# First slot's weights sent a step ahead of their split, routing reads ordered ahead, and the plan of the rest drawn up in the second slot

## The chip, the core and the metric

The kernel runs on one core of a Trainium2 chip. The metric is device time in microseconds (us) of one execution. Engines are named as the profile names them: PE (matmuls), PEld (its weight loads), DVE (vector), ACT (scalar), POOL (GpSimd) and SP (which here only issues transfers and reads indices into registers; its queue is SPq in the profile).

## The reference

Three stages in a row, all in float32:

```
# 1. gated linear attention, B=4, H=8, S=768, D=48
f = 1 / (1 + exp(-f_logit))
state = f[t] * state + k[t] (x) v[t];   y[t] = q[t] @ state
# 2. dense layer over 3072 tokens of 384 (d_ff 2048)
x = softplus(y @ w_in) @ w_out
# 3. mixture of 8 experts, one expert for each token (F=1024)
e = argmax(x @ w_gate + modality_bias[modality_id]);  p = softmax(...)[e]
out = p * (relu(x @ w1[e]) @ w2[e])
```

## The kernel before, in words

**Stages one and two.** Attention and the dense layer run in 128 steps, `NG` = 8 groups of 384 tokens by 16 blocks of 128 hidden columns. Each step is an `up` (L573), a softplus on ACT and DVE, and a `down` (L653) into three accumulators `x2ps0` to `x2ps2`. When a group is done, `route1` reads the three accumulators: the gate's logits `lg` on DVE, and the rows of tokens `rows`, of which parts 0 and 2 are read on ACT and part 1 on DVE. `route2` then finds each token's expert and its place, and POOL scatters the rows into a buffer in HBM, `xs`, sorted by expert (L724).

**Stage three** works in slots. A slot is up to 256 tokens of one expert, and `seq` lists them: four "first" slots, whose experts are known from `plan_first` before the last group is done, and then the "rest", which `plan_rest` finds once all tokens are counted. Slots are numbered from 0 here, so slot 3 is the last of the first four and slot 4 the first of the rest. A slot has eight blocks f0 to f7 of `m_up`, nine matmuls each into one of `HBUF` = 4 PSUM buffers `h` (L1115). A block's result is read twice, by ACT (`hh`, L1117) and by DVE (`hl`, L1118), and only then is its buffer free for the block four later. Two `m_down` follow, 24 matmuls each (L1138), and `m_out` scales the accumulator on ACT (`o`, L1147) and scatters it on POOL (L1148).

**Weights.** While a slot runs, the next slot's weights are fetched (`m_weights`): eight loads of 384 KB, turn by turn of w1 and w2, each into one of `RAW` = 6 buffers `raw` (two for slot 0). Each is then split in two: ACT casts it to a high half (`w1h`, `w2h`, L1009), DVE subtracts for a low half (`w1l`, `w2l`, L1010). I call the eight loads of a slot A to H in the order of issue: A, C, E and G are w1, B, D, F and H are w2. Between B and C, SP issues the load of the slot's token rows, `xr` (L984). Before the loads SP reads the expert's number (`woff`, L994), and before `xr` the row's offset (`roff`, L982). Both come out of the plan on DVE. For a slot of the rest, `xr` also waits for every scatter of rows and for all eight "pads" to have landed (`after` in `m_load`); pads are the transfers of 388 KB by which POOL closes each expert's rows (`pad_rows`, L1209).

**Order.** Each engine runs its instructions in the order that a scheduler wrote when the program was built, from the kernel's program order and from its own idea of when data arrive. `follow(a, b)` adds an order without a wait: a stands behind b if both are on one engine. `at(s, f)` runs f at step s of the dense layer. `m_slots` is given calls to place: `(2, 2): then` draws up the plan of the rest in block 2 of slot 2.

Of the kernel before, what the change touches and what calls it, by code (L numbers as in the profile page):

```python
# [7 lines left out]
F32 = mybir.dt.float32  # L8
# [3 lines left out]
AF = mybir.ActivationFunctionType  # L12
ALU = mybir.AluOpType
# [5 lines left out]
NT, DM, DFF = 3072, 384, 2048  # L19
E, FE = 8, 1024  # L20
TG = 384
NG = NT // TG
# [3 lines left out]
SLOT = 256  # L26
# [9 lines left out]
PRE = 4  # L36
# [3 lines left out]
TAIL = "uaduue"  # L40
WPOS = 1
PADROW = E * CAP
PAIR0, PAIR1 = NF, NF * (NG - 1)
RW = 388
BIG = 65536.0
WS = 256.0
# [5 lines left out]
def moe_chain(ctx, tc, qT, kT, fT, vp, w_in, w_out, mod, w_gate, mbias, w1, w2, out):  # L52
    nc = tc.nc
# [23 lines left out]
    x2ps = [ps_x.tile([128, 512], F32, name=f"x2ps{j}") for j in range(3)]  # L77


    def follow(ins, other):  # L80

        tc.add_manual_dep(ins.ins, other.name,
                          mybir.DependencyInfo(mybir.DependencyClass.NoSync, mybir.DependencyReason.DATA),
                          reason="first steps first")

    def behind(ins):
        follow(ins, anchor[0])

    marks = {}
# [315 lines left out]
    biasT = cp.tile([128, 24, 8], F32, name="biasT")  # L405
# [261 lines left out]
    def sm(nm, shape, dt=F32):  # L667
        return gp.tile(shape, dt, tag=nm, name=nm)

    def route1(G, j):  # L670
        if j == 0:
            rt[G] = {"lg": sm("lg", [128, 3, 8]), "rows": gp.tile([128, 3, RW], F32, tag="rows", name="rows", bufs=1)}
        lg, rows = rt[G]["lg"], rt[G]["rows"]
        nc.vector.scalar_tensor_tensor(lg[:, j, :], x2ps[j][:, DM:DM + 8], 1.0 / WS, biasT[:, 3 * G + j, :],
                                       op0=ALU.mult, op1=ALU.add)
        if j == 1:
            nc.vector.tensor_scalar(rows[:, j, 0:DM], x2ps[j][:, 0:DM], 1.0 / WS, None, op0=ALU.mult)
        else:
            nc.scalar.activation(rows[:, j, 0:DM], x2ps[j][:, 0:DM], AF.Copy, scale=1.0 / WS)  # L679

    def route2(G):
        d = rt[G]
# [55 lines left out]
    def pick(nm, num, w, offs):  # L738
# [16 lines left out]
        nc.vector.tensor_reduce(row, tmp, axis=AX.X, op=ALU.add)  # L755
        nc.vector.tensor_scalar(roff, row, float(PADROW), None, op0=ALU.add)
        return woff, roff, beg, end
# [34 lines left out]
    def halves(num, offs):  # L792
# [15 lines left out]
        nc.vector.tensor_copy(pw, ph[:, :, 0])  # L808
        nc.vector.tensor_scalar(pr, ph[:, :, 1], float(PADROW), None, op0=ALU.add)
        return pw, pr  # L810
# [48 lines left out]
    def late_consts():  # L859
# [9 lines left out]
        nc.gpsimd.iota(etab, pattern=[[0, 2], [1, 8]], base=0, **it)  # L869
        nc.gpsimd.iota(rows0, pattern=[[0, 2], [CAP, 8]], base=-PADROW, **it)  # L870
        nc.gpsimd.iota(snum, pattern=[[0, 1]], base=0, channel_multiplier=1, allow_small_or_imprecise_dtypes=True)
# [3 lines left out]
    def pad_out():  # L875
        behind(nc.scalar.dma_start(xs[PADROW:PADROW + SLOT, :].rearrange("(p j) w -> p j w", j=2),
                                   padt.unsqueeze(1).to_broadcast([128, 2, RW])))
# [3 lines left out]
    def at(s, f):  # L881
        extra.setdefault(s, []).append(f)
# [32 lines left out]
    for u in range(4, 33):  # L915
        G, j = divmod(u, 4)
        t = 3 * u - 10 if u < 8 else 4 * u - 19
# [63 lines left out]
    def m_load(s, where, i, n):  # L981
        ro = nc.sync.value_load(plans[where][1][i:i + 1, 0:1], min_val=0, max_val=PADROW)  # L982
        xr = xrp.tile([128, 2, RW], F32, tag="xr", name="xr")[:, 0:n, :]
# [8 lines left out]
    def m_weights(s, woff, i, whole):  # L992

        wo = nc.sync.value_load(woff[i:i + 1, 0:1], min_val=0, max_val=E - 1)  # L994
        pl = m1p[s % 2]
        names = ("w1h", "w1l", "w2h", "w2l")
        w1h, w1l, w2h, w2l = wts[s] = [pl.tile([128, 3 * FE], F32R, tag=n, name=n) for n in names]
        ops = []
        for n in range(4):
            for src, hi, lo in ((w1, w1h, w1l), (w2, w2h, w2l)):  # L1000
                def op(n=n, src=src, hi=hi, lo=lo):
                    c = slice(768 * n, 768 * n + 768)
                    rows = src[bass.ds(wo, 1), :, c].rearrange("o p f -> p (o f)")
                    if whole and src is w1:
                        nc.sync.dma_start(hi[:, c].bitcast(F32), rows)
                        return
                    t = rawp.tile([128, 768], F32, tag="raw", name="raw")
                    nc.sync.dma_start(t, rows)
                    nc.scalar.copy(hi[:, c], t)  # L1009
                    nc.vector.tensor_tensor(lo[:, c], t, hi[:, c].bitcast(F32), op=ALU.subtract)  # L1010
                ops.append(op)
        return ops

    def p_load(s):
        xr = xrp.tile([128, 2, RW], F32, tag="xr", name="xr")[:, 0:1, :]
        for n in range(2):
            ro = nc.sync.value_load(plans["rest"][3][0:1, n:n + 1], min_val=0, max_val=PADROW)
            ins = nc.sync.dma_start(xr[HALF * n:HALF * n + HALF, 0, :], xs[bass.ds(ro, HALF), :]).ins
# [83 lines left out]
    def m_up(s, f):  # L1102
        d = sl[s]
        t = d["t"]
        w1h, w1l = (t.rearrange("p (k f) -> p k f", k=3) for t in wts[s][0:2])
        if f == 0:
            d["hh"] = mp.tile([128, NF2, SLOT], F32R, tag="hh", name="hh")
            d["hl"] = mp.tile([128, NF2, SLOT], F32R, tag="hl", name="hl")
        if d["n"] == 2:
            hp = ps_h.tile([128, TG], F32, tag="h", name="h")  # L1110
            fs = slice(128 * f, 128 * f + 128)
            n = 0
            for kd in range(3):
                for w, x in ((w1h, 0), (w1h, 1), (w1l, 0)):
                    nc.tensor.matmul(hp[:, 0:SLOT], w[:, kd, fs], t[x][:, kd, :], start=(n == 0), stop=(n == 8))  # L1115
                    n += 1
            nc.scalar.activation(d["hh"][:, f, :], hp[:, 0:SLOT], AF.Relu)  # L1117
            nc.vector.scalar_tensor_tensor(d["hl"][:, f, :], hp[:, 0:SLOT], 0.0, d["hh"][:, f, :].bitcast(F32),  # L1118
                                           op0=ALU.max, op1=ALU.subtract)
        elif f % 2 == 0:  # L1120
            w1f = wts[s][0].bitcast(F32).rearrange("p (k f) -> p k f", k=3)
            hp = ps_h.tile([128, 2, 128], F32, tag="h", name="h")
            for i in range(2):
                fs = slice(128 * (f + i), 128 * (f + i) + 128)
                for kd in range(3):
                    nc.tensor.matmul(hp[:, i, :], w1f[:, kd, fs], t[:, kd, :], start=(kd == 0), stop=(kd == 2))
            hh, hl = d["hh"][:, f:f + 2, 0:128], d["hl"][:, f:f + 2, 0:128]
            nc.scalar.activation(hh, hp, AF.Relu)
            nc.vector.scalar_tensor_tensor(hl, hp, 0.0, hh.bitcast(F32), op0=ALU.max, op1=ALU.subtract)
# [26 lines left out]
    seq = [("first", i, 2) for i in range(NPRE)] + [("rest", i, 2 if i < NA else 1) for i in range(NSTAT)]  # L1156
# [4 lines left out]
    def m_slots(items, last):  # L1161

        for x, (s, it) in enumerate(items):
            nxt = items[x + 1] if x + 1 < len(items) else None
            wops = []
            if nxt:
                wops = m_fetch(*nxt)
            for f in range(NF2):
                if it[0] == "pair":
                    if f % 2 == 0:  # L1170
                        p_up(s, f)
                elif f >= ahead or s:
                    m_up(s, f)
                if (s, f) in last:
                    last[s, f]()
                if wops:
                    wops.pop(0)()
                if f == 6 and nxt:
                    m_T(nxt[0], (0,) if it[2] == 2 else (0, 1))
            if x + 2 < len(items) and items[x + 2][1][0] == "pair":  # L1180
                for op in p_weights(items[x + 2][0], w1):
                    op()
            for j in range(it[2]):
                if it[0] == "pair":
                    p_down(s)
                else:
                    m_down(s, j)
                if j == 0 and it[2] == 2 and nxt:
                    m_T(nxt[0], (1,))
            if s == len(seq) - 3:  # L1190
                follow(nc.gpsimd.drain(), gone[-1])
# [14 lines left out]
    def pad_rows(e):  # L1206
# [5 lines left out]
            tc.declare_no_dep(ins, other, reason="rows of different experts")  # L1212
        pads.append(ins)

    def pre():
        plans["first"] = plan_first()
        for i in range(NPRE - 1):
            m_load(i, "first", i, 2)
        for n, op in enumerate(m_fetch(0, seq[0])):
            at(16 * (NG - 1) + PRE + 1 + n, op)  # L1220

    ffn(0, 16 * (NG - 1) + 3)
    for p in (ap1, ap2, ps_r, ps_h):
# [31 lines left out]
    seq = list(enumerate(seq))  # L1255
# [2 lines left out]
        for e in range(E):  # L1258
            pad_rows(e)

    m_slots(seq, {(0, 3): final, (1, 2): lambda: route2(NG - 1), (1, 4): ready, (2, 2): then, (6, 3): limits})
    def slow():
        sp = cp
        ma, mb = m1p[0], m1p[1]
# [182 lines left out]
```

## Time and profile before

| | us |
|---|---|
| three runs | 814.3, 816.16, 819.37 |
| median | 816.16 |
| profiled execution, whole | 814.61 |
| its span, first to last instruction | 812.9 |
| PE busy | 786.5 (97%) |
| DVE busy | 633.5 (78%) |
| ACT busy | 530.4 (65%) |

Times in the text are in us from the start of the span. The profiled execution lies at the lower end of the three runs, 1.55 us under their median. The four first slots lie in 556 to 635 us of the span; the matmuls end at 807.5.

### The profile page before, as it was taken

How to read it: one execution, taken by the hardware profiler on the slowest of the kernel's cores; microseconds unless marked ns; L12 is line 12 of the kernel's file. 1: busy time of each engine (PE TensorE's matmuls, PEld its weight loads, DVE VectorE, ACT ScalarE, POOL GpSimd, SP SyncE). 2: the span in 40 equal slices, each digit the busy share in tenths (PEclk: the TensorE clock that was granted, in tenths of full speed). 3: DMA queues.
4: the chain of work that ended last, by engine and by line, in shares of the span. 5: the costliest groups of instructions: out<-in, count | busy, mean ns of one | idle time of the engine just before them, and what ended most of it. 6: DMA issues, size and time to landing. Idle time of an engine off the chain costs nothing.

```text
span 812.9 us, 16010 instructions
## 1 busy us (share of the span) xinstructions
PE 786.5 (97%) x5878; PEld 730.8 (90%) x5878; DVE 633.5 (78%) x1265; ACT 530.4 (65%) x1057; POOL 64.9 (8%) x86
## 2 busy tenths in 40 slices
PE   4899999999999999999999999999999999999997
PEld 4656568999999999999999999989999999999987
DVE  6899999998888888888888866888886766666131
ACT  5787797767766676777676665566775656655242
POOL 2000000200010010010010010100042111000010
PEclk9999999999999999999999999999999999999999
DMA  8794221321132132122221010055598976673980
GB/s 292 255 328 140 59 67 44 91 73 54 45 95 58 45 98 58 51 85 61 62 75 38 23 38 8 30 161 171 200 352 298 309 226 216 213 225 119 366 311 16
DMA packets 53976, 110.84 MB, mean 136 GB/s; under 512 B 7655, under 2 KB 27930, under 8 KB 53888
## 3 DMA queue, kind: packets, MB, share of 16 engines
q1 hardware_dynamic: 48768, 96.61, 37.2%
q0 software_dynamic: 4160, 12.67, 4.2%
q8 instruction: 48, 0.79, 0.4%
q10 hardware_dynamic: 960, 0.44, 0.2%
q14 instruction: 40, 0.33, 0.1%
HBM read 91.92 MB, written 13.65 MB: 130 GB/s over the span
## 4 chain that ended last, share of the span: by engine, by line
PE 49%; DVE 23%; ACT 10%; issue 10%; DMA 7%; SPq 1%; POOL 1%; POOLq 0%; DVEq 0%; ACTq 0%
PE x2ps L653 11%; PE h L573 11%; PE x2ps L1138 10%; PE h L1115 10%; DVE l L637 3%; DVE w L636 2%; DMA raw<-in_w_dram 2%; ACT e L633 1%; DVE f L110 1%; PE r L206 1%; ACT e L622 1%; DVE lo L640 1%; DVE am L214 1%; DVE l L639 1%; ACT r L623 1%
## 5 line engine op out<-in xcount | busy, mean ns | idle before, releaser
L573 PE MATMUL h<-xh,wih 128*128 128x384 f32 x336 | 118.4, 352 | 1.2 <-DVE e L587 1.2
L653 PE MATMUL x2ps<-woh,hi 128*128 128x392 f32 x336 | 115.3, 343 | 1.8 <-ACT hi L612 1.5
L653 PE MATMUL x2ps<-wol,hi 128*128 128x392 f32 x336 | 114.5, 341 | 0.0
L573 PE MATMUL h<-xh,wil 128*128 128x384 f32 x336 | 113.5, 338 | 0.0
L653 PE MATMUL x2ps<-woh,lo 128*128 128x392 f32 x336 | 113.4, 341 | 0.0
L573 PE MATMUL h<-xl,wih 128*128 128x384 f32 x336 | 113.3, 337 | 0.0
L1115 PE MATMUL h<-thl,w1h 128*128 128x256 f32 x528 | 96.5, 284 | 0.0
L1010 DVE TENSOR_TENSOR w2l<-raw,w2h 128x768 fp32r<-128x768 f32 x56 | 53.2, 951 | 38.8 <-ACT w2h L1009 18.0
L1115 PEld LDWEIGHTS h<-thl,w1h 128*128 128x128 f32 x528 | 82.0, 190 | 0.0
L638 ACT CAST hi<-l 128x768 fp32r<-128x768 f32 x48 | 40.0, 834 | 54.1 <-DVE l L637 42.5
L1115 PE MATMUL h<-thl,w1l 128*128 128x256 f32 x264 | 74.3, 282 | 0.0
L1138 PE MATMUL x2ps<-w2h,hh 128*128 128x384 f32 x208 | 71.0, 341 | 0.2 <-ACT rows L679 0.2
L1138 PE MATMUL x2ps<-w2h,hl 128*128 128x384 f32 x208 | 70.1, 337 | 0.8 <-DVE hl L1118 0.8
L1138 PE MATMUL x2ps<-w2l,hh 128*128 128x384 f32 x208 | 69.9, 336 | 0.0
L573 PEld LDWEIGHTS h<-xh,wih 128*128 128x128 f32 x336 | 63.0, 188 | 4.9 <-DVE e L587 2.0
L724 POOL DMA_INDIRECT xs<-rows,pos x24 | 27.1, 1129 | 504.4 <-DVE w L635 166.3
L653 PEld LDWEIGHTS x2ps<-woh,hi 128*128 128x128 f32 x336 | 63.0, 188 | 3.2 <-ACT hi L612 2.6
L653 PEld LDWEIGHTS x2ps<-woh,lo 128*128 128x128 f32 x336 | 63.0, 188 | 0.5
L573 PEld LDWEIGHTS h<-xl,wih 128*128 128x128 f32 x336 | 63.3, 188 | 0.0
L653 PEld LDWEIGHTS x2ps<-wol,hi 128*128 128x128 f32 x336 | 63.1, 188 | 0.0
L573 PEld LDWEIGHTS h<-xh,wil 128*128 128x128 f32 x336 | 63.0, 188 | 0.0
L1010 DVE TENSOR_TENSOR w1l<-raw,w1h 128x768 fp32r<-128x768 f32 x48 | 45.8, 954 | 21.9 <-ACT w1h L1009 21.3
(275 smaller groups left out, 1826.7 us busy)
## 6 DMA issues: line engine op xcount, KB each, us to landing
raw<-in_w_dram SPq DMA_DIRECT2D x104, 384.0 KB
f<-in_f_dram SPq DMA_DIRECT2D x28, 192.0 KB
k<-in_k_dram SPq DMA_DIRECT2D x28, 192.0 KB
q<-in_q_dram SPq DMA_DIRECT2D x28, 192.0 KB
xr<-xs SPq DMA_DIRECT2D x12, 388.0 KB
v<-in_v_dram SPq DMA_DIRECT2D x32, 144.0 KB
w1h<-in_w_dram SPq DMA_DIRECT2D x12, 384.0 KB
xf<-y SPq DMA_DIRECT2D x48, 72.0 KB
```

The lines of the kernel that those rows point to most:

```text
L110: nc.vector.tensor_tensor_scan(d["f"], d["f"], clampt.to_broadcast([128, TG]), 1.0 if first else fl[:, n:n + 1], op0=ALU.mult, op1=ALU.min)
L206: nc.tensor.matmul(pa[h][:, cs], d["k"][64 * h:64 * h + 64, cs], d["q"][64 * h:64 * h + 64, cs], start=(c == 0), stop=True, skip_group_che ...
L214: marks["mask"] = nc.vector.tensor_tensor(am, pa[h][:, 0:TG].rearrange("p (c t) -> p c t", c=3), mask.unsqueeze(1).to_broadcast([128, 3, 1 ...
L573: nc.tensor.matmul(hp, w, x, start=(n == 0), stop=(n == len(terms) - 1))
L636: nc.vector.tensor_tensor(w, w, e, op=ALU.subtract)
L637: nc.vector.tensor_tensor(g, r, g, op=ALU.add)
L638: nc.scalar.copy(hi, g)
L653: nc.tensor.matmul(x2ps[j][:, 0:DM + 8], g[:, ts], w, start=(i == 0 and n == 0), stop=(i == NF - 1 and n == len(terms) - 1))
L724: ins = nc.gpsimd.indirect_dma_start(out=xs, out_offset=bass.IndirectOffsetOnAxis(ap=pos[:, j:j + 1], axis=0), in_=rows[:, j, :], in_offse ...
L1010: nc.vector.tensor_tensor(lo[:, c], t, hi[:, c].bitcast(F32), op=ALU.subtract)
L1115: nc.tensor.matmul(hp[:, 0:SLOT], w[:, kd, fs], t[x][:, kd, :], start=(n == 0), stop=(n == 8))
L1138: nc.tensor.matmul(acc[:, 0:DM], g[:, f, ts], w[:, f, :], start=(f == 0 and n == 0), stop=(f == NF2 - 1 and n == 2))
```

## The change

It has three parts. (1) In slot 0's fetch, a load and its split are two calls, and the split is placed one step behind the load (`m_weights` returns `parts`, `pre` places both). (2) `route1` keeps its reads in `marks`, and in slot 0 blocks f4 to f6 of `m_up` are ordered behind them: `hh` and `hl` of f4 behind the reads of part 0, `hl` of f5 behind those of part 1, `hh` and `hl` of f6 behind those of part 2. (3) `plan_rest` is called in block 6 of slot 1, not in block 2 of slot 2.

```diff
--- before.py
+++ after.py
@@ -40,6 +40,7 @@
 TAIL = "uaduue"
 WPOS = 1
 PADROW = E * CAP
+LATE = 4
 PAIR0, PAIR1 = NF, NF * (NG - 1)
 RW = 388
 BIG = 65536.0
@@ -667,16 +668,21 @@
     def sm(nm, shape, dt=F32):
         return gp.tile(shape, dt, tag=nm, name=nm)
 
+    marks["route"] = []
+
     def route1(G, j):
         if j == 0:
             rt[G] = {"lg": sm("lg", [128, 3, 8]), "rows": gp.tile([128, 3, RW], F32, tag="rows", name="rows", bufs=1)}
         lg, rows = rt[G]["lg"], rt[G]["rows"]
-        nc.vector.scalar_tensor_tensor(lg[:, j, :], x2ps[j][:, DM:DM + 8], 1.0 / WS, biasT[:, 3 * G + j, :],
-                                       op0=ALU.mult, op1=ALU.add)
+        ins = [nc.vector.scalar_tensor_tensor(lg[:, j, :], x2ps[j][:, DM:DM + 8], 1.0 / WS, biasT[:, 3 * G + j, :],
+                                              op0=ALU.mult, op1=ALU.add)]
         if j == 1:
-            nc.vector.tensor_scalar(rows[:, j, 0:DM], x2ps[j][:, 0:DM], 1.0 / WS, None, op0=ALU.mult)
+            ins.append(nc.vector.tensor_scalar(rows[:, j, 0:DM], x2ps[j][:, 0:DM], 1.0 / WS, None, op0=ALU.mult))
+            eng = (0, 0)
         else:
-            nc.scalar.activation(rows[:, j, 0:DM], x2ps[j][:, 0:DM], AF.Copy, scale=1.0 / WS)
+            ins.append(nc.scalar.activation(rows[:, j, 0:DM], x2ps[j][:, 0:DM], AF.Copy, scale=1.0 / WS))
+            eng = (0, 1)
+        marks["route"] = [(j, e, x) for e, x in zip(eng, ins)] + [y for y in marks["route"] if y[0] != j]
 
     def route2(G):
         d = rt[G]
@@ -1006,8 +1012,15 @@
                         return
                     t = rawp.tile([128, 768], F32, tag="raw", name="raw")
                     nc.sync.dma_start(t, rows)
-                    nc.scalar.copy(hi[:, c], t)
-                    nc.vector.tensor_tensor(lo[:, c], t, hi[:, c].bitcast(F32), op=ALU.subtract)
+
+                    def parts():
+                        nc.scalar.copy(hi[:, c], t)
+                        nc.vector.tensor_tensor(lo[:, c], t, hi[:, c].bitcast(F32), op=ALU.subtract)
+
+                    if s:
+                        parts()
+                    else:
+                        return parts
                 ops.append(op)
         return ops
 
@@ -1114,9 +1127,13 @@
                 for w, x in ((w1h, 0), (w1h, 1), (w1l, 0)):
                     nc.tensor.matmul(hp[:, 0:SLOT], w[:, kd, fs], t[x][:, kd, :], start=(n == 0), stop=(n == 8))
                     n += 1
-            nc.scalar.activation(d["hh"][:, f, :], hp[:, 0:SLOT], AF.Relu)
-            nc.vector.scalar_tensor_tensor(d["hl"][:, f, :], hp[:, 0:SLOT], 0.0, d["hh"][:, f, :].bitcast(F32),
-                                           op0=ALU.max, op1=ALU.subtract)
+            two = [None, nc.scalar.activation(d["hh"][:, f, :], hp[:, 0:SLOT], AF.Relu)]
+            two[0] = nc.vector.scalar_tensor_tensor(d["hl"][:, f, :], hp[:, 0:SLOT], 0.0, d["hh"][:, f, :].bitcast(F32),
+                                                    op0=ALU.max, op1=ALU.subtract)
+            if s == 0 and f >= LATE and f < LATE + 3:
+                for j, e, x in marks["route"]:
+                    if j == f - LATE:
+                        follow(two[e], x.ins)
         elif f % 2 == 0:
             w1f = wts[s][0].bitcast(F32).rearrange("p (k f) -> p k f", k=3)
             hp = ps_h.tile([128, 2, 128], F32, tag="h", name="h")
@@ -1212,12 +1229,15 @@
             tc.declare_no_dep(ins, other, reason="rows of different experts")
         pads.append(ins)
 
+    turn = []
+
     def pre():
         plans["first"] = plan_first()
         for i in range(NPRE - 1):
             m_load(i, "first", i, 2)
         for n, op in enumerate(m_fetch(0, seq[0])):
-            at(16 * (NG - 1) + PRE + 1 + n, op)
+            at(16 * (NG - 1) + PRE + 1 + n, lambda op=op: turn.append(op()))
+            at(16 * (NG - 1) + PRE + 2 + n, lambda: turn.pop(0)())
 
     ffn(0, 16 * (NG - 1) + 3)
     for p in (ap1, ap2, ps_r, ps_h):
@@ -1258,7 +1278,7 @@
         for e in range(E):
             pad_rows(e)
 
-    m_slots(seq, {(0, 3): final, (1, 2): lambda: route2(NG - 1), (1, 4): ready, (2, 2): then, (6, 3): limits})
+    m_slots(seq, {(0, 3): final, (1, 2): lambda: route2(NG - 1), (1, 4): ready, (1, 6): then, (6, 3): limits})
     def slow():
         sp = cp
         ma, mb = m1p[0], m1p[1]
```

The scheduler makes of it the following. On PE, DVE, ACT and SP nothing stands in another place before slot 0's blocks.

ACT in slot 0. `hh_6544<-h_...` are the blocks f0 to f7, `thl` is slot 1's transposed tokens, `rows` are route1's reads. Before, from f3 on:

```order
L1117 ACTIVATE hh_6544<-h_6640 128x256
L1117 ACTIVATE hh_6544<-h_6664 128x256
L1117 ACTIVATE hh_6544<-h_6680 128x256
L1117 ACTIVATE hh_6544<-h_6696 128x256
L1099 CAST thl_6712<-r_6713 128x512
L1117 ACTIVATE hh_6544<-h_6720 128x256
L679 ACTIVATE rows_6653<-x2ps0_89 128x384
L1099 CAST thl_6712<-r_6765 128x256
L679 ACTIVATE rows_6653<-x2ps2_91 128x384
```

and in the change:

```order
L1130 ACTIVATE hh_6544<-h_6640 128x256
L1130 ACTIVATE hh_6544<-h_6680 128x256
L1112 CAST thl_6712<-r_6713 128x512
L1130 ACTIVATE hh_6544<-h_6720 128x256
L683 ACTIVATE rows_6653<-x2ps0_89 128x384
L1130 ACTIVATE hh_6544<-h_6664 128x256
L1112 CAST thl_6712<-r_6765 128x256
L683 ACTIVATE rows_6653<-x2ps2_91 128x384
L1130 ACTIVATE hh_6544<-h_6696 128x256
```

f4 (`h_6664`) and f6 (`h_6696`) moved behind the reads of x2ps0 and x2ps2; f5 and f7 stayed ahead.

SP at slot 4's fetch. `pwoff` and `proff` are the plan's numbers for the one slot of pairs, read into registers long before their use; `raw_7469` is load A, `raw_7485` B, `raw_7512` C, `raw_7528` D, `raw_7544` E; `xr_7510` is slot 4's token rows. Before:

```order
L1026 TENSOR_LOAD pwoff_7237
L994 TENSOR_LOAD woff1_7262
L1008 DMA raw_7469<-in_w1_dram 128x768
L1008 DMA raw_7485<-in_w2_dram 128x768
L982 TENSOR_LOAD roff1_7263
L984 DMA xr_7510<-xs_70 128x776
L1008 DMA raw_7512<-in_w1_dram 128x768
```

and in the change:

```order
L1039 TENSOR_LOAD pwoff_7087
L1030 TENSOR_LOAD proff_7088
L1000 TENSOR_LOAD woff1_7112
L1014 DMA raw_7469<-in_w1_dram 128x768
L1014 DMA raw_7485<-in_w2_dram 128x768
L988 TENSOR_LOAD roff1_7113
L990 DMA xr_7510<-xs_70 128x776
L1014 DMA raw_7512<-in_w1_dram 128x768
```

Only reads of the plan's numbers were added (`pwoff` and `proff` are read twice each); `xr` still stands between B and C.

ACT at the end of slot 2 and the start of slot 3. `o_7403` and `o_7437` are slot 2's two outputs, `thl_7355` slot 3's tokens, `hh_7455<-h_7457` slot 3's block f0, `h_7473` f1, `h_7489` f2, `h_7516` f3. Before:

```order
L1147 ACTIVATE o_7403<-x2ps1_90,xr_6138 128x384
L1099 CAST thl_7355<-r_7408 128x256
L1147 ACTIVATE o_7437<-x2ps2_91,xr_6138 128x384
L1009 CAST w1h_7451<-raw_7469 128x768
L1117 ACTIVATE hh_7455<-h_7457 128x256
L1009 CAST w2h_7453<-raw_7485 128x768
L1117 ACTIVATE hh_7455<-h_7473 128x256
L1117 ACTIVATE hh_7455<-h_7489 128x256
L1117 ACTIVATE hh_7455<-h_7516 128x256
L1009 CAST w1h_7451<-raw_7512 128x768
```

and in the change:

```order
L1017 CAST w1h_7451<-raw_7469 128x768
L1164 ACTIVATE o_7403<-x2ps1_90,xr_6138 128x384
L1112 CAST thl_7355<-r_7408 128x256
L1017 CAST w1h_7451<-raw_7512 128x768
L1017 CAST w1h_7451<-raw_7544 128x768
L1164 ACTIVATE o_7437<-x2ps2_91,xr_6138 128x384
L1017 CAST w2h_7453<-raw_7485 128x768
L1130 ACTIVATE hh_7455<-h_7457 128x256
L1017 CAST w2h_7453<-raw_7528 128x768
L1130 ACTIVATE hh_7455<-h_7473 128x256
```

The casts of A, C, E and B moved ahead of slot 3's block f0; before, A alone stood ahead of it.

## Rows read from the trace of the kernel before

**Rows 1.** The page, first part: busy us and share of PE.
```profile
PE 786.5 (97%) x5878; PEld 730.8 (90%) x5878; DVE 633.5 (78%) x1265; ACT 530.4 (65%) x1057; POOL 64.9 (8%) x86
```
**Rows 2.** Waits of PE, 535 to 640 us: total us, times, longest.
```profile
PE x2ps L653 <- ACT hi L612: 1.5, 2, 1.2
PE x2ps L1138 <- DVE hl L1118: 0.8, 1, 0.8
```
**Rows 3.** Busy time by stretch, slot 3: us, PE, PEld, DVE, ACT, POOL, clock, DMA share, GB/s.
```profile
616.85:635.40 18.55, 17.76 (x128) 17.43 (x128) 12.63 (x20) 11.97 (x22) 2.18 (x2) 1.00 0.98 345
```
**Rows 4.** Timeline, first slot's weights arriving: start, us, instruction, [idle before <-releaser].
```profile
538.12 0.83 ACT L1009 CAST w1h<-raw 128x768 fp32r<-128x768 f32 x1 [1.88 <-DMA raw<-in_w_dram]
...
542.35 0.45 PE L653 MATMUL x2ps<-woh,hi 128*128 128x392 f32 x1 [1.22 <-ACT hi L612]
```
**Rows 5.** Timeline of ACT and PE at slot 0's end, 570 to 573 us.
```profile
570.35 0.58 ACT L1099 CAST thl<-r 128x512 fp32r<-128x512 f32 x1
...
571.71 0.44 PE L1097 MATMUL r<-ident,xr 128*128 128x128 f32 x2 [0.50 <-DVE thl L1100]
572.36 0.44 PE L1138 MATMUL x2ps<-w2h,hh 128*128 128x384 f32 x1 [0.22 <-ACT rows L679]
```
**Rows 6.** Waits of SP's queue, 598 to 620 us.
```profile
SPq L1026 <- DVE sel L749: 13.8, 1, 13.8
```
**Rows 7.** Timeline of DVE and SP at slot 4's fetch: woff, loads A and B, xr.
```profile
613.68 0.13 DVE L750 CAST woff<-sel 17x1 int32<-17x1 f32 x1
...
614.75 0.92 SPq L1008 DMA_DIRECT2D raw<-in_w_dram  x2
...
616.73 0.33 SPq L984 DMA_DIRECT2D xr<-xs  x1
```
**Rows 8.** POOL's pads on the timeline; DMA queues 607 to 613: packets, MB, share.
```profile
600.16 2.90 POOL L1209 DMA_DIRECT2D xs<-padt  x4 [6.69 <-DMA xs<-rows,pos]
...
608.46 0.68 POOL L1209 DMA_DIRECT2D xs<-padt  x1 [0.80 <-issue]
...
q0 software_dynamic: 479, 1.62, 74.5%
```
**Rows 9.** Busy time by stretch while the pads move (columns as in rows 3).
```profile
602.00:613.00 11.00, 11.00 (x82) 10.92 (x81) 10.67 (x52) 5.74 (x13) 6.52 (x8) 1.00 0.87 312
```
**Rows 10.** Timeline of ACT in slot 3: casts of A, B and E, blocks, an output.
```profile
616.87 0.58 ACT L1147 ACTIVATE o<-x2ps,xr 128x384 f32<-128x384 f32 x1 [3.56 <-PE x2ps L1138]
618.18 0.84 ACT L1009 CAST w1h<-raw 128x768 fp32r<-128x768 f32 x1 [0.72 <-DMA raw<-in_w_dram]
618.92 0.38 ACT L1117 ACTIVATE hh<-h 128x256 fp32r<-128x256 f32 x1
...
625.69 0.84 ACT L1009 CAST w1h<-raw 128x768 fp32r<-128x768 f32 x1 [1.16 <-DMA raw<-in_w_dram]
```
**Rows 11.** Timeline of DVE in slot 3: a split, then a block's hl.
```profile
619.05 0.96 DVE L1010 TENSOR_TENSOR w1l<-raw,w1h 128x768 fp32r<-128x768 f32 x1 [4.59 <-ACT w1h L1009]
619.92 0.42 DVE L1118 SCALAR_TENSOR_TENSOR hl<-h,hh 128x256 fp32r<-128x256 f32 x1
```
**Rows 12.** Timeline of PE in slot 3: block f4 begins; the wait in its first m_down.
```profile
620.93 0.40 PE L1115 MATMUL h<-thl,w1h 128*128 128x256 f32 x2
...
629.44 0.34 PE L1138 MATMUL x2ps<-w2l,hh 128*128 128x384 f32 x1
630.57 0.44 PE L1138 MATMUL x2ps<-w2h,hl 128*128 128x384 f32 x1 [0.79 <-DVE hl L1118]
```
**Rows 13.** Timeline and stretches of PE after a pause: first matmuls, last matmul, clock.
```profile
10.21 1.51 PE L133 MATMUL r<-ident,wih_raw 128*128 128x128 f32 x6 [10.21 <-DVE wih_raw L283]
...
14.22 1.70 PE L306 MATMUL x2ps<-v,kt 128*64 128x96 f32 x40
...
17.38 0.88 PE L133 MATMUL r<-ident,wih_raw 128*128 128x128 f32 x6
...
807.15 0.34 PE L1138 MATMUL x2ps<-w2h,hl 128*128 128x384 f32 x1
...
810.00:812.90 2.90, 0.00 (x0) 0.00 (x0) 0.00 (x0) 0.00 (x0) 0.00 (x0) 0.51 0.10 33
```

## The prediction

> **What bounds the kernel now.** I read the page's first part first [rows 1]: PE is busy for 786.5 of 812.9 us. A change that adds no matmul and removes none can therefore only gain where PE stands still, so the next view is the waits of PE over the stretch that the change touches, the end of the dense layer and the four first slots [rows 2]. There is little: 1.2 us once in the dense layer, for ACT's `hi`, and 0.8 us once in slot 3's `m_down`, for `hl`. The two smaller ones at the end of slot 0, 0.50 and 0.22 us, are in the timeline [rows 5]. Together that is 2.7 us, 0.3% of the time. The stretches then tell what else is full: in slot 3 PE runs at clock 1.00 and the DMA engines are busy for 0.98 of the time, at 345 GB/s [rows 3]. So in slot 3 a load can't come sooner unless the loads ahead of it do. What can be lost is larger than what can be gained: whatever makes PE wait for these loads is lost whole.
>
> **Part 1, the split one step behind its load.** The wait that it points at is the 1.88 us that ACT spent before its first cast of slot 0's weights, waiting for the load; PE's 1.22 us wait for `hi` comes behind it [rows 4]. But ACT, DVE, PE and SP have the same order before slot 0's blocks as before: the scheduler had already placed each of these splits where the new program order puts it. The cast stands where it stood, so the wait stays: 0 gained, 0 lost.
>
> **Part 2, f4 to f6 behind the reads.** ACT now has `thl` ahead of f6's `hh`. Before, the cast of `thl` began at 570.35, the transposes behind it waited 0.50 us for the `thl` that DVE finishes from it, and the first `m_down` matmul waited 0.22 us for ACT's read of `rows` [rows 5]. One block's read less ahead of them is 0.38 us (the shape's row in slot 3 [rows 10]); the later read of f4 has time, since its consumer is the same `m_down` that starts after the reads. Bounds are 0 and 0.5, the wait itself; I take 0.25.
>
> **Part 3, the plan in slot 1.** Before, `woff` came at 613.68, because the plan was placed late; SP stood 13.8 us at L1026 for the plan [rows 6], issued A and B from 614.75 on and `xr` at 616.73 [rows 7]. Now the plan's numbers should be there some 6 us earlier, at about 607 or 608 (the plan is four blocks and two `m_down` earlier in program order, but it still waits for the last group's counts). A and B, two loads, can go at once. `xr` can't: it stands on SP between B and C, and it waits until all eight pads have landed. The pads are issued by POOL from 600.16 to 608.46, and the software queue that carries them is still at 74.5% and moves 1.62 MB in 607 to 613 [rows 8]. While they move, the DMA engines are busy for 0.87 of the time [rows 9]. So behind B the queue of SP stops until the pads are down, and C to H stand behind it.
>
> When does `xr` go (I call it t0)? With the pads undisturbed they are down by 613.0 at the latest, and with 0.4 us for the offset's read and the issue, t0 is 613.4. A and B are 786 KB, 2.28 us at 345 GB/s [rows 3], and they now move while the pads do. The idle 0.13 of the 11 us in 602 to 613 is 1.43 us [rows 9], which takes up part of it. So the pads are 0.85 to 2.28 us late. I take t0 = 615.0, with bounds of 613.4 (no delay) and 616.7 (no earlier than before).
>
> The Trainium skill, "DMA: Bandwidth & Descriptors", section "Issuing engines are not separate DMA queues", states that transfers from SP and from POOL end on the same 16 engines and interleave. That speaks against this change: by it A and B take their 2.28 us out of the pads, t0 is 615.7 and the sum 0.7 us higher; if the queues were apart, it would be 1.6 us lower. No row of before shows pads beside loads of weights.
>
> That alone would cost nothing, for A to H are needed in slot 4 only. What makes it cost is the order of ACT: the scheduler, which thinks the loads early, has put the casts of A, C, E and B ahead of slot 3's f0. ACT is in order, so f0's `hh` waits for load E, which stands behind `xr`. PE goes on for f0 to f3 and then needs f0's buffer for f4, which began at 620.93 before [rows 12].
>
> E's cast came 8.96 us behind `xr` before (616.73 [rows 7] to 625.69 [rows 10]), with A and B still moving ahead of it. Now these are down, which takes off 2.28: E = t0 + 6.7 = 621.7. The least that I can defend is t0 + 5.7: the time of three loads (C, D and E) less one, 2.28, and 3.43 from issue to landing, as A took (614.75 [rows 7] to 618.18 [rows 10]). The bounds are then 613.4 + 5.7 = 619.1 and 616.7 + 8.96 = 625.7.
>
> From E's cast to f4, along ACT and then DVE, by pitches of before [rows 10, 11]: E's cast 0.74 (618.18 to 618.92), slot 2's output 0.58, B's cast to its split 0.87 (618.18 to 619.05), the split to the next `hl` 0.87 (619.05 to 619.92), and f0's `hl` 0.42; `hh` of f0 is 0.38 on ACT beside the split. That is 3.48 us. So f4 starts at 625.2, against 620.93: **PE loses 4.3 us**, bounds 1.7 (622.6) and 8.3 (629.2). The instant is set by transfers, so part 2's 0.25 us is used up in this wait and counts only where there is none. The 0.79 us wait in slot 3's `m_down` [rows 12] came from splits of slot 4's weights in front of an `hl`; half of these now lie behind PE's stop, and I take it away whole (bounds 0 and 0.79).
>
> **The clock after the stop.** PE stops for about as long as at the end of the kernel, where the last matmul starts at 807.15 and the granted clock of 810.0 to 812.9 is 0.51 [rows 13], the lower of the two levels, 1.2 GHz. At the start of the kernel PE has stood still for 10.21 us, and six transposes of 128x128 take 1.51 us; the same six take 0.88 at 17.38, and the forms in between (from 14.22) run at the higher level, 2.4 GHz [rows 13]. So the 4.01 us between 10.21 and 14.22 cost 4.01 x (1 - 0.88/1.51) = 1.7 us. If the clock holds, it is 0. The stop that I forecast is shorter than the one at the start and of the order of that at the end; I take the middle, 0.85.
>
> The Trainium skill, "TensorE: Matmul & The Clock Gate", "Part 1: The HAM clock gate", has it that the lower clock is the default and that activity releases it; by that a stopped PE restarts slowly, with the full 1.7 us, and the sum is 819.8. The rows show both levels but no stop of 4 us between busy stretches.
>
> **Sum**, against the profiled execution: 814.61 + 4.3 - 0.79 + 0.85 = 818.97, so **819**. That execution is 1.55 us below the median of the runs, 816.16; on the median's scale the same sum is 820.5, which the range has to take in. The forecast's own range is 814.61 + 1.7 - 0.79 = 815.5 to 814.61 + 8.3 + 1.7 = 824.6.
>
> **Rivals.**
> First, **the loads come in time and the change works** (the faster side). Then f0's `hh` is not late, `m_down`'s wait goes and part 2 counts: 814.61 - 0.25 - 0.79 = 813.6. It needs E's cast by 620.93 - 3.48 = 617.45, so t0 by 611.7 even with the short 5.7 us. For it: 0.13 of the DMA engines is free [rows 9], and the last pad is issued at 608.46 [rows 8]. Against it: the pads' queue is busy up to 613 [rows 8], and A and B come on top. 0.12.
>
> Second, **the stop is long and PE restarts at the low clock** (slower by more than the forecast). The point from which it decides is a t0 of 616 or more: A and B are served ahead of the pads, `xr` goes no earlier than before, E keeps its 8.96 us, and the stop is 8.3 us, nearly as long as the one at the start, with 1.7 us of clock behind it: 814.61 + 8.3 - 0.79 + 1.7 = 823.8, on the median's scale 825.4. For it: DMA at 0.98 in slot 3 leaves no room to catch up [rows 3]. Against it: the gaps in 602 to 613, and two loads are then down that were ahead of E before. 0.10.
>
> Third, **the change does nothing**, part 3 like part 1: `xr` and the plan come as before, ACT's casts are late and yet not in the way. It gives 814.6. The order of ACT excludes it, unless the loads come in time, so its chance lies in the first.
>
> The forecast keeps 0.78.
>
> **How the numbers follow.** About 1%, 8 us, is what a measurement of this kernel can tell from no change. The range reaches from 815.5, the forecast's low end, to 824.5, its high end, which takes in the median's scale and most of the second rival; left out are the first rival (0.12) and the top of the second (some 0.06). Faster by over 1% would need 808, more than all the idle time of the touched stretch: 0.01. Slower by over 1% needs 824.3: nearly all of the second rival, 0.09. Between them 0.90.
>
> **What the profile after would show.** Part 1: ACT's 1.88 us and PE's 1.22 us waits still stand near 538 and 542. Part 2: the wait for `thl` at 571.7 shorter by about 0.25. Part 3: A's issue at 608 or so, `xr` at 613.4 to 616.7, a wait of SP ahead of `xr` that ends with a DMA; ACT idle ahead of C's and E's casts for the loads; E's cast at 619 to 626; f4 of slot 3 late by 3.48 us behind that, with `hl` or `hh` of f0 as the releaser; a granted clock under 1.00 in the few us after. I am wrong if A is issued no sooner than before, if f0's `hh` goes ahead of E's landing, or if the pads are down before 611.7.

## The result

| | before | after |
|---|---|---|
| median of six runs each | 815.44 | 825.73 |
| lowest to highest | 814.3 to 819.37 | 821.78 to 827.24 |
| profiled execution, whole | 814.61 | 826.29 |
| its span | 812.9 | 824.6 |

After over before is 1.0107, with a 95% interval of 1.0072 to 1.0141: 8.7 us slower (5.9 to 11.5), twice the 4.4 us that I forecast. The direction and the mechanism held; the stop is nearly as long as the second rival had it.

### The profile page after: what moved, and what is told of

It reads as the page before. It is cut to its first block, busy times and chain, and to the rows that moved or that the text cites. A ratio compares the mean times of both kernels' runs of the same rounds, so it can differ in the third digit from the quotient of the medians.

```text
span 824.6 us, 16008 instructions
## 1 busy us (share of the span) xinstructions
PE 790.0 (96%) x5878; PEld 732.8 (89%) x5878; DVE 633.1 (77%) x1265; ACT 530.1 (64%) x1057; POOL 65.3 (8%) x86
## 4 chain that ended last, share of the span: by engine, by line
PE 59%; issue 15%; DVE 12%; DMA 7%; ACT 4%; POOL 1%; POOLq 1%; SPq 1%; ACTq 0%; DVEq 0%
PE h L574 17%; PE x2ps L654 17%; PE h L1128 8%; PE x2ps L1155 8%; PE r L207 2%; PE r L183 2%; DMA k<-in_k_dram 2%; PE r L195 2%; POOL out_dram L1165 1%; DMA woh_raw<-in_w_in_dram 1%; PE r L134 1%; DMA xs<-rows,pos 1%; DMA raw<-in_w_dram 1%; PE r L154 1%; DVE f L111 1%
```

## The profile after

Waits of PE, 535 to 660 us (total us, times, longest), against [rows 2]:

```profile
PE h L1128 <- DVE hl L1131: 7.5, 1, 7.5
PE x2ps L654 <- ACT hi L613: 1.1, 2, 0.9
PE r L1110 <- DVE thl L1113: 0.3, 1, 0.3
PE x2ps L1155 <- ACT rows L683: 0.2, 1, 0.2
```

The first line is new: one stop of 7.5 us, released by the `hl` of slot 3's f0. The 0.8 us wait in slot 3's `m_down` is gone; the other three are the old ones.

ACT's timeline around it, against [rows 10]:

```profile
618.83 0.83 ACT L1017 CAST w1h<-raw 128x768 fp32r<-128x768 f32 x1 [6.65 <-DMA raw<-in_w_dram]
...
625.22 0.83 ACT L1017 CAST w1h<-raw 128x768 fp32r<-128x768 f32 x1 [4.82 <-DMA raw<-in_w_dram]
628.91 0.83 ACT L1017 CAST w1h<-raw 128x768 fp32r<-128x768 f32 x1 [2.85 <-DMA raw<-in_w_dram]
629.64 0.57 ACT L1164 ACTIVATE o<-x2ps,xr 128x384 f32<-128x384 f32 x1
630.12 0.82 ACT L1017 CAST w2h<-raw 128x768 fp32r<-128x768 f32 x1
630.84 0.38 ACT L1130 ACTIVATE hh<-h 128x256 fp32r<-128x256 f32 x1
```

The three casts are A, C and E. ACT stands idle ahead of each, for its load, and f0's `hh` comes only at 630.84. PE's timeline (slot 3 begins, f4, slot 4 begins), against [rows 12]:

```profile
620.16 0.40 PE L1128 MATMUL h<-thl,w1h 128*128 128x256 f32 x2
...
632.32 0.80 PE L1128 MATMUL h<-thl,w1h 128*128 128x256 f32 x2 [7.47 <-DVE hl L1131]
632.91 0.42 PE L1128 MATMUL h<-thl,w1l 128*128 128x256 f32 x1
...
635.62 0.39 PE L1128 MATMUL h<-thl,w1h 128*128 128x256 f32 x2
...
647.16 0.41 PE L1128 MATMUL h<-thl,w1h 128*128 128x256 f32 x2
```

SP's timeline and its waits there (against [rows 6, 7]):

```profile
614.19 0.99 SPq L1014 DMA_DIRECT2D raw<-in_w_dram  x2
620.49 0.33 SPq L990 DMA_DIRECT2D xr<-xs  x1
```

```profile
SPq L1039 <- DVE stmp L754: 5.6, 1, 5.6
SPq L990 <- DMA out_dram<-o,xr: 4.1, 1, 4.1
```

SP's wait for the plan fell from 13.8 to 5.6 us, and a new one of 4.1 us stands ahead of `xr`. PE by stretch (us, PE, PEld, DVE, ACT, POOL, clock, DMA share, GB/s):

```profile
620.00:622.00 2.00, 1.99 (x16) 1.79 (x16) 1.10 (x4) 0.41 (x2) 1.09 (x1) 1.00 0.27 29
622.00:630.00 8.00, 2.85 (x25) 2.65 (x23) 1.19 (x2) 1.93 (x3) 0.00 (x0) 0.92 0.97 356
630.00:632.00 2.00, 0.00 (x0) 0.00 (x0) 1.76 (x3) 2.00 (x5) 1.09 (x1) 0.50 0.17 48
632.00:636.00 4.00, 3.68 (x19) 3.68 (x20) 4.00 (x8) 3.25 (x7) 0.00 (x0) 0.56 0.70 244
```

While SP waits, the DMA engines run dry (29 GB/s in 620 to 622); during the stop PE's clock falls to the lower level (0.50 in 630 to 632), and the first 3.3 us behind it are run at that.

**Where the time went.** The two profiled spans are 11.7 us apart. Before's slot 3 and slot 4 began at

```profile
616.67 0.40 PE L1115 MATMUL h<-thl,w1h 128*128 128x256 f32 x2
...
635.23 0.40 PE L1115 MATMUL h<-thl,w1h 128*128 128x256 f32 x2
```

so slot 3 took 18.56 us, and now 647.16 - 620.16 = 27.00: 8.44 more. From slot 0's first `m_down` matmul to the last matmul (I call this **the slots**) it is 242.9 us (575.78 to 818.69) against 234.8 (572.36, [rows 5], to 807.15, [rows 13]): 8.1 more, so all else in the slots gave 0.3 back. Another 3.4 us come ahead of slot 0's end. I don't count these to the change. They begin at 26 to 31 us, where PE waited 2.19 us for `wif` (1.03 before) and ran part of 30 to 40 us at the lower clock (granted 0.83, before 1.00), with code that no part touches and that PE, ACT and DVE run in the same order. Of the eleven experiments that hold parts 1 and 2, seven have 1.00 throughout 20 to 60 us; the one with these two parts alone falls to 0.83 in 30 to 40 us, three others in 40 to 50. They begin slot 0 anywhere from 0.75 us ahead of before's 556.48 (555.73) to 5.85 us behind it (562.33), and the kernel with these two parts alone is at 1.0000 of before. So I compare profiles by the slots, and kernels by the ratio.

## The experiments

Theory: ACT's order, which puts casts of late loads ahead of slot 3's blocks, makes the stop (DVE's order follows it: the splits of C, E and B stand ahead of f0's `hl`). Rivals: parts 1 and 2 lose as well; the early plan costs by itself, through the pads or the late loads. Each edit is against the change, unless it says otherwise.

| | ratio to before, interval | slots, us | longest wait of PE in slots 3 and 4, us |
|---|---|---|---|
| the change | 1.0107 (1.0072 to 1.0141) | 242.9 | 7.5 |
| plan alone | 1.0091 (1.0061 to 1.0121) | 245.0 | 7.6 |
| parts 1 and 2 | 1.0000 (0.9976 to 1.0023) | 235.0 | 1.0 |
| casts behind | 1.0026 (1.0002 to 1.0050) | 239.3 | 2.4 |
| `xr` behind F | 1.0035 (1.0015 to 1.0055) | 238.4 | 2.2 |
| casts at the end | 1.0035 (1.0008 to 1.0061) | 238.9 | 1.0 |
| both | 1.0039 (1.0019 to 1.0058) | 239.1 | 2.6 |
| plan at (1, 7) | 1.0066 (1.0044 to 1.0087) | 240.9 | 4.7 |
| `xr` buffer free | 1.0071 (1.0048 to 1.0094) | 241.0 | 3.6 |
| plan at (2, 0) | 0.9988 (0.9972 to 1.0004) | 236.3 | 0.4 |
| loads first | 1.0009 (0.9990 to 1.0028) | 234.8 | 1.0 |
| order of before, slot 3 | 1.0033 (1.0016 to 1.0050) | 237.1 | 1.5 |
| order of before, slots 3 and 4 | 0.9999 (0.9981 to 1.0017) | 235.0 | 0.2 |

**Plan alone** (before, with `(1, 6): then`). 

> The kernel before with part 3 alone. Theory (the whole loss is PE's stop in slot 3, made by part 3's order of ACT and the wait of xr): a stop of 7 to 8 us before slot 3's f4, released by f0's hl; from slot 0's first m_down to the last matmul 242 to 243 us against 234.8 before; time 8 to 9 us above the kernel before. Rival (a part of the loss, the 3.4 us that the profile of the change shows ahead of slot 0's end, is made by parts 1 and 2): the same stop, but only about 5 us above the kernel before in total.

Its stop is 7.6 us and the slots take 245.0, 2 us more than the upper end of what was expected; about 0.9 of that is the clock, which stayed low for 5.3 us behind the stop, not 3.3. Part 3 alone has the whole loss.

**Parts 1 and 2** (`(2, 2): then`). 

> The change with the plan back in block 2 of slot 2, so parts 1 and 2 alone. Theory: no stop in slot 3, the wait for thl at the end of slot 0 shorter by 0.2 us, the rest as before; time within 1 us of the kernel before. Rival (parts 1 and 2 lose what the profile shows ahead of slot 0's end): 3 us above it.

No difference beyond the interval, 1.9 us either way (ratio 1.0000). Waits of PE, 535 to 660 us:

```profile
PE x2ps L654 <- ACT hi L613: 1.4, 2, 1.2
PE x2ps L1155 <- DVE hl L1131: 1.0, 1, 1.0
PE r L1110 <- DVE thl L1113: 0.3, 1, 0.3
```

Part 1 moved nothing: the 1.2 us wait stands. Part 2 took the wait for `thl` from 0.50 to 0.34 and gives nothing that can be measured.

**Casts behind.**

The lines that do it (x is the cast, y the split, `marks["two"]` the latest `hl` and `hh`; the rest of the edit only gives them names):

```
+                        if s == NPRE:
+                            follow(x, marks["two"][1].ins)
+                            follow(y, marks["two"][0].ins)
```

> The change, with ACT's casts and DVE's splits of slot 4's weights ordered behind slot 3's blocks, the cast of load A behind f0, B behind f1 and so on; loads, xr and the plan stay as in the change. Theory (the order of ACT turns the late load into a stop of PE): no stop at f4, slot 3 takes 18 to 18.6 us against 26.9 in the change, time that of the kernel before or up to 1 us under it. Rival (the late loads stop PE whatever ACT does): slot 3 still 4 us or more longer than before, since the loads C to H still stand behind xr's wait.

Half a miss: the stop at f4 went, but slot 3 took 21.4 us, with a stop of 2.4 us at f7, which needs f3's buffer, and 0.9 us in `m_down`. In this order C's cast stands ahead of f3's `hh`, and ACT waits there (ACT's timeline):

```profile
620.89 0.39 ACT L1133 ACTIVATE hh<-h 128x256 fp32r<-128x256 f32 x1
625.69 0.83 ACT L1017 CAST w1h<-raw 128x768 fp32r<-128x768 f32 x1 [4.41 <-DMA raw<-in_w_dram]
626.43 0.38 ACT L1133 ACTIVATE hh<-h 128x256 fp32r<-128x256 f32 x1
```

The same thing with C and f3 in place of E and f0. It did not tell theory and rival apart; the last two experiments do.

**`xr` behind F** (`ops[2]` becomes `ops[6]` for slot 4 in `m_fetch`). 

> The change, with slot 4's xr moved on SP from between B and C to between F and G; ACT's order stays that of the change, with the casts of A, C, E and B ahead of slot 3's f0. Theory (E comes late because it stands behind xr's wait): E is issued some 4 us sooner, lands 5 to 7 us sooner, and the stop falls from 7.6 to 0 to 3 us, the time to 0 to 4 us above the kernel before. Rival (E is late because the DMA engines are full with the pads): the stop stays over 5 us.

The stop is 2.2 us, with the same order on ACT up to slot 3's f1. Against slot 3's start E was issued 6.0 us sooner than in the change (613.90 - 617.82 against 622.28 - 620.16) and cast 4.8 us sooner (621.81 - 617.82 = 3.99 against 8.75). So most of E's lateness comes from standing behind `xr`; the rest stays, for E now took 7.9 us from issue to cast, beside the pads, where it had taken 6.6.

**Casts at the end** (C to H behind f7). 

> The change, with ACT's casts and DVE's splits of the loads C to H of slot 4 ordered behind the last block, f7, of slot 3 (A's and B's stay). In the run with casts each behind its block C's cast still stood ahead of f3's hh, and PE still waited there. Theory (only a cast of a late load ahead of an hh stops PE): no stop over 0.5 us in the blocks of slot 3, slot 3 takes 17.7 to 18.6 us, 234 to 235.5 us from slot 0's first m_down to the last matmul (change: 242.9, before: 234.8). Rival (the late loads cost PE 2 to 4 us whatever ACT's order is, in slot 3 or at the start of slot 4): 237 to 239 us.

The slots come out where the rival had them, at 238.9. Slot 3 has no stop in its blocks but 1.2 us at its start for `thl`, which stands behind A's cast; slot 4 pays 2.7 us in three waits for `hl`. The next slot's loads are late under an order written for early ones: A of slot 5 went at 635.67, 8.5 us behind H of slot 4. SP's order had changed too, with 14 reads of later slots' numbers between these two loads; what the longer hold on the `raw` buffers adds is not shown. The loss moved.

**Both** (the third and fourth in one). 

> Both cures in one: casts of slot 4's weights each behind its block of slot 3, and xr moved behind F. Theory: C and E now land before their turn, no stop, slot 3 17.7 to 18.6 us, 234 to 235.5 us from slot 0's first m_down to the last matmul, time within 1 us of the kernel before. Rival (each cure leaves its own remainder, the cast order 2.8 us and the loads 3.7 us): 237 to 239 us.

Also a miss: no stop in the blocks, but 2.6 us in `m_down`, for f7's `hh`. Ahead of that `hh` ACT has the casts of G (632.36) and of slot 5's A (635.31, after 1.62 us of waiting for its load). Both loads went late: `xr` was issued at 623.17, and G only at 629.11, for SP now had eight reads of later slots' numbers between them. So this run does not show the two cures at work alone.

**Plan at (1, 7).** 

> The change with the plan one block later, in block 7 of slot 1. The scheduler then puts the casts of A, C and B ahead of slot 3's f0, but E's behind f1; C came 3.7 us ahead of E. Theory (the cast that stands ahead of f0 sets the stop): first stop 3.5 to 4.5 us, another 0.5 to 1.5 us at f5 or f6 for E, 238.5 to 241 us from slot 0's first m_down to the last matmul. Rival (the stop is set by the time at which the plan lets the loads go): 7 us or more, 242 to 243 us.

One stop of 4.7 us. The scheduler put E's cast behind f1 and left C's ahead of f0, and the stop follows C.

**`xr` buffer free.**

The new lines; the scatter then takes its offsets from `ix`:

```
+        ix = xr.bitcast(I32)[:, j, 385:386]
+        if s == 1:
+            ix = gp.tile([128, 1], I32, tag="ix", name="ix", bufs=2)
+            nc.vector.tensor_copy(ix, xr.bitcast(I32)[:, j, 385:386])
```

> The change, with slot 1's scatter indices copied out of its xr buffer (two copies on DVE), so that slot 4's xr, which takes that buffer, no longer waits for slot 1's output scatters and waits for rows and pads only. Theory (in the change the last that xr waits for is slot 1's second scatter, which stands behind the pads on POOL's queue): xr is issued 2 to 3 us sooner, the stop falls from 7.6 to 4.5 to 5.5 us, 239 to 241 us. Rival (the pads are the last, as the prediction had it): xr at the same place, stop over 7 us, 242 to 243 us.

SP's waits and timeline:

```profile
SPq L990 <- DMA xs<-padt: 2.1, 1, 2.1
```

```profile
620.84 0.33 SPq L990 DMA_DIRECT2D xr<-xs  x1
```

Slot 3 begins at 622.75 here, so `xr` goes 1.91 us ahead of that, where it was 0.33 us behind it in the change: 2.2 us sooner, and now the pads release it. What `xr` waited for in the change was slot 1's output scatter, which reads the buffer that slot 4's `xr` takes. The stop falls to 3.6 us, further than expected: E's cast also came only 7.5 us behind `xr` (628.31 - 620.84), not 8.4.

**Plan at (2, 0).** 

> The change with the plan in block 0 of slot 2, two blocks ahead of the kernel before and two behind the change. The scheduler then leaves A alone ahead of slot 3's f0, C ahead of f3 (before: ahead of f4). Theory (an early plan costs nothing as long as ACT's order keeps late casts behind the blocks): no stop over 1.5 us in slot 3, which takes 18 to 19.5 us; 234.3 to 236 us from slot 0's first m_down to the last matmul; time within 1.5 us of the kernel before. Rival (an early plan costs by itself, through the loads A and B beside the pads): 237 to 239 us, 2 to 4 us above the kernel before.

As before in time, with a wait of 0.4 us in slot 3. The slots are 1.5 us longer, just over what was expected; 0.9 of it is one wait of PE in slot 1, for DVE's `ends` (L794). But this run does not test an early plan. SP waited for it as long as before:

```profile
SPq L1039 <- DVE sel L755: 13.8, 1, 13.8
```

and A went 1.98 us ahead of slot 3's start (617.86 against 619.84), before 1.92, in the change 5.97. What an early plan costs by itself is told by the last run, where A goes 6.46 us ahead (612.49 against 618.95).

**Loads first** (parts 1 and 2; slot 0's first two loads ahead of two of the `xr`). 

> Parts 1 and 2 with part 1 made to act on the transfers: slot 0's first two loads of weights go out ahead of the token rows xr of slots 1 and 2, which stood before them on SP. The plan stays in slot 2. The first load lands some 2 us sooner. Theory: ACT's 1.9 us wait ahead of the first cast goes, and with it PE's 1.2 us wait for hi near 542: up to 1.2 us (0.15%) under the kernel before, at the edge of what the rounds can tell. Rival: the scheduler, which sees the loads go sooner, sets the casts sooner as well (the first cast is now one step ahead on ACT), and the wait stays at 1 to 2 us.

The rival holds: the cast moved one step forward with the load and waits as before, and the time is that of before (1.0009).

```profile
535.57 0.84 ACT L1017 CAST w1h<-raw 128x768 fp32r<-128x768 f32 x1 [1.69 <-DMA raw<-in_w_dram]
```

**Order of before, slot 3** (the casts A to H put back by `follow`, and their splits; plan, `xr` and SP's order up to load F as in the change; behind F, SP has six reads of later slots' numbers ahead of G, so G goes later). 

> The change, with ACT's and DVE's order in slot 3 written as in the kernel before: slot 4's casts A behind slot 2's last output, B behind f0, C behind f3, D behind f4, E behind f5, F behind f6. The plan, SP's order and xr's wait stay those of the change, so C to H go no sooner than in it. Theory (the late loads were there before as well, and only the order of ACT made a stop of them): no stop over 1.2 us in slot 3, which takes 18 to 19 us against 27.0 in the change and 18.56 before. Slot 4 may lose 0 to 3 us, since DVE's order there still has one more split of slot 5 ahead of its first block than before. In total 234.5 to 238 us from slot 0's first m_down to the last matmul (change 242.9). Rival (the early plan and the wait of xr cost by themselves): slot 3 over 21 us.

SP's timeline and PE's waits, 600 to 662 us:

```profile
616.40 0.33 SPq L991 DMA_DIRECT2D xr<-xs  x1
```

```profile
PE h L1136 <- ACT thl L1120: 1.5, 1, 1.5
PE h L1136 <- DVE thl L1121: 0.2, 1, 0.2
```

Slot 3 takes 17.6 us, 1.0 less than before, though `xr` goes 0.55 us behind slot 3's start (615.85), no sooner than in the change. The 1.5 us stand at slot 4's start: there C's cast of slot 5 had moved ahead of `thl`.

**Order of before, slots 3 and 4** (also C and E of slot 5). 

> As the run with the order of before in slot 3, and slot 5's casts of C and E (ACT, and their splits on DVE) put back too: C behind slot 4's second thl, E behind slot 4's f1. ACT then has the order of the kernel before in slots 3 and 4, with all three parts of the change in. Theory: the 1.5 us wait for thl at slot 4's start goes as well; slots 3 and 4 take 17.5 to 18.2 us each, 233.8 to 235.5 us from slot 0's first m_down to the last matmul (before 234.8), time within 1 us of the kernel before, at best 1 us under it. Rival (some 2 us stay, whatever the order): 236.5 us or more.

PE's waits, 600 to 662 us, and its timeline at the start of slots 3 and 4:

```profile
PE h L1141 <- DVE thl L1125: 0.2, 1, 0.2
```

```profile
618.95 0.40 PE L1141 MATMUL h<-thl,w1h 128*128 128x256 f32 x2
...
636.68 0.40 PE L1141 MATMUL h<-thl,w1h 128*128 128x256 f32 x2
```

Slot 3 takes 17.7 us, the slots 235.0, the ratio is 0.9999. The loads were as late as in the change: `xr` went 0.32 us behind slot 3's start (619.27), and C's and E's casts (ACT's timeline)

```profile
624.09 0.84 ACT L1018 CAST w1h<-raw 128x768 fp32r<-128x768 f32 x1 [0.30 <-DMA raw<-in_w_dram]
628.01 0.84 ACT L1018 CAST w1h<-raw 128x768 fp32r<-128x768 f32 x1 [0.57 <-DMA raw<-in_w_dram]
```

waited for their loads until 5.14 and 9.06 us behind that start (in the change 5.06 and 8.75), and PE did not stop. With all three parts in and the order of the casts and splits put back, nothing is left of the loss. That shows the cause: the order, not the loads or the early plan. ACT and DVE were put back together, so the share of each is not shown. No version tried beats the kernel before by more than its interval.

## Why the prediction was right and where it was off

- **The sum:** the way was right, the size was not: 4.4 us forecast, 8.7 (5.9 to 11.5) measured. Added to 814.61 that is 823.3, near the top of the range (824.5); the plain median of the change, 825.73, lies 1.2 us past it. The terms as measured, 7.5 for the stop, 1.5 for the clock and 0.8 off for `m_down`, make 8.2, against the 8.4 by which slot 3 grew. Only the wide bounds took that in.
- **What bounds the kernel, and the order of ACT as the lever:** right. The stop stands at slot 3's f4, behind f0's `hl`, and putting back the order of casts and splits takes the loss away.
- **Parts 1 and 2:** right; 0 for part 1, a wait shorter by 0.16 us for part 2 (I took 0.25), which shows in no total.
- **t0 = 615.0:** a step that failed, by 2 us: 620.49 less the 3.4 us of the profile's start is 617.1, just past my upper bound of 616.7. A went at 614.19, which is 610.8 on that scale, not 608: SP read four of the plan's numbers for the slot of pairs first (608.8 to 613.0). That did not set `xr`, for SP then stood 4.1 us more ahead of it. The 0.4 us that I gave the offset's read and the issue is shown by no row; SP read the offset at 615.2, ahead of the wait, so it did not count. What hurt is the end of `xr`'s wait. I named the pads; it was slot 1's output scatter, queued behind the pads on POOL, whose `xr` buffer slot 4 takes. With that wait gone the pads ended it 2.2 us sooner.
- **E = t0 + 6.7:** the other step that failed, by 1.7 us. It was 628.91 - 620.49 = 8.42, near the 8.96 of before. I took 2.28 us off because A and B were no longer ahead. They were done before `xr` went, as I had it, but the engines had run dry by then, C to H came together at 356 GB/s, and the lag stayed; why is not shown. Counted from slot 3's start, E's cast came after 8.75 us in the change and after 9.02 (625.69 - 616.67) before, C's after 5.06 (625.22 - 620.16) and 5.73 (622.40 - 616.67, in ACT's timeline of before):

```profile
622.40 0.84 ACT L1009 CAST w1h<-raw 128x768 fp32r<-128x768 f32 x1 [0.89 <-DMA raw<-in_w_dram]
```

Each of these four casts waited for its load. **C came 0.7 us sooner and E 0.3; what was new was the order that took them for early.** Had I left E where before shows it, the stop would have been 625.69 + 3.48 - 620.93 = 8.2 us, next to my upper bound of 8.3. How the engines share out C to H among themselves was not tried.
- **E to f4 = 3.48:** right; 632.32 - 628.91 = 3.41.
- **The stop, 4.3:** 7.5, inside the bounds 1.7 to 8.3.
- **The wait in `m_down`, 0.79:** gone, as said.
- **The clock, 0.85:** 1.5. Five groups of three matmuls took 635.62 - 632.32 = 3.30 us, and at the full clock such a group takes 0.355 (five groups 617.03 to 618.80 in the trace of before), so 1.77. The full term, 1.7, would have been close here. It rested on the durations of the kernel's first matmuls alone: the profile gives their stretch, 10 to 14 us, a granted clock of 1.00. The Trainium skill, "TensorE: Matmul & The Clock Gate", "Part 1: The HAM clock gate", states that the lower clock is the default and that activity releases it. The trace agrees: 0.50 in the stop and 0.56 in the 4 us behind it.
- **The rivals:** "in time" is excluded by ACT's waits of 4.82 and 2.85 us. The long stop with a slow clock is close to what came, though by its size: its t0 over 616 held, its reason (A and B served ahead of the pads) was not the one that ended the wait.

The Trainium skill's "DMA: Bandwidth & Descriptors", "Issuing engines are not separate DMA queues", states that transfers started by different engines run on the same 16 DMA engines and interleave, by which A and B would make the pads late. The packets in the traces agree with it: the last packet of the pads ended 4.25 us ahead of slot 3's start before, 3.59 in the change and 2.60 with the buffer free, so 0.7 and 1.65 us later. That A and B are the reason was not isolated; in the change the delay is under my bounds of 0.85 to 2.28.

## What to carry to other kernels

Where an order is fixed at build time from modelled arrival times, an earlier issue can be paid with later work: read which reader of a transfer moved ahead of what, and price it with the arrival that the trace of before shows, not with one that the change is hoped to bring. Ask of every transfer in the queue what it waits for, the last reader of its buffer among them; the loads behind it share that wait. And a cure that moves the late reader only a little can hand the loss on, to the next block, `m_down` or the next slot. After such an edit read the order of every engine again: in five of these runs (casts behind, casts at the end, both, and the two with the order of before) it also moved reads on SP ahead of loads.

## What was not expected of the hardware

- Profiles of the same code can be some 3 us apart by 60 us. The matmul that came at 60 us before came 2.6 us later in the change and 3.5 later in the run with the buffer free. PE's wait for `wif` was 1.03, 2.19 and 1.64 us in these, and the granted clock fell to 0.83 in 30 to 40 us in the second and in 40 to 50 us in the third.
- The clock's price did not follow the length of the stop. Behind the 3.6 us stop of the run with the buffer free (f4 at 631.72) the stretches read (columns as above)

```profile
632.00:636.00 4.00, 4.00 (x20) 4.00 (x21) 3.60 (x7) 2.69 (x7) 0.00 (x0) 0.50 0.71 244
636.00:637.00 1.00, 1.00 (x6) 1.00 (x6) 0.61 (x2) 0.35 (x1) 0.00 (x0) 0.50 0.87 316
637.00:638.00 1.00, 1.00 (x9) 1.00 (x9) 0.68 (x1) 0.26 (x1) 0.00 (x0) 0.81 0.91 363
```

so PE ran at the lower level for 5.3 us (eight groups, 631.72 to 637.01; at 0.355 they are 2.84, so 2.4 us were lost), longer than the 3.3 us behind the 7.5 us stop. Behind the 2.2 us stop of the run with `xr` behind F (f4 at 625.23) it was 0.59 and 0.55:

```profile
625.00:627.00 2.00, 1.77 (x9) 1.78 (x9) 2.00 (x4) 0.85 (x2) 0.00 (x0) 0.59 1.03 345
627.00:629.00 2.00, 2.00 (x12) 2.00 (x12) 1.07 (x3) 1.98 (x4) 0.00 (x0) 0.55 0.95 359
```

Behind the 7.6 us stop of the plan alone it was low for 5.3 us (629.47 to 634.73). Behind the 2.4 us stop of the run with the casts behind (f7 at 627.90) it was not low at all:

```profile
628.00:629.00 1.00, 1.00 (x9) 1.00 (x10) 1.00 (x3) 1.00 (x3) 0.00 (x0) 1.00 0.70 169
```

The upper bound of 1.7 us that I gave this term held in the change (1.5) and not in others (2.4 in these two of 5.3 us). What decides it is not shown.
